# Seven products in place of eight for the first matrix product of two batches, other pairs of token tiles, and a new order of the whole program

## The chip, the cores and the metric

The kernel runs on one core of a Trainium2 chip. The core has a matmul engine (TensorE, PE in the profile, with its weight loads as PEld), three elementwise engines (VectorE or DVE, ScalarE or ACT, GpSimd or POOL) and a queue engine (SyncE, SP) that issues most DMAs. Each engine executes its own instructions strictly in the order in which the program issues them; engines wait for one another by semaphores. The metric is the device time of one execution in microseconds; lower is better.

## The reference

```
q, k, v: (batch 8, heads 12, sequence 448, head size 64), float32
q_n = q / (norm(q) + 1e-6);  k_n = k / (norm(k) + 1e-6)
attn = softmax(q_n @ k_n^T / 0.1)                 # per head, 448 x 448
x = (attn @ v), heads side by side                # 3584 tokens x 768
h = x @ w_in                                      # w_in: 768 x 2048
g = h * clip(h + 3, 0, 6) / 6
out = g @ w_out                                   # w_out: 2048 x 768
```

## The kernel before

Work is done by pairs of heads: 8 batches x 6 pairs = 48, numbered 0 to 47 and called heads below. For each the kernel loads q and k of two heads (`load_qk`, one item j each), squares them (`square`, L228 on ACT, L230 on DVE or POOL), sums the squares (`reduce`, L242), makes the reciprocal norms with four small ACT instructions (`norms`, L258 to L261), scales (`normalise`, L273), transposes by PE or by DMA (`transposes`, `crossbar`), and copies k into a padded tile (`copy_k`, `copy_k3`). `scores` (L418, L421) multiplies keys by queries: the two heads of a pair lie in the upper and lower 64 rows of the array and run side by side, three groups of 128 keys each and a fourth group, M, that holds the last 64 keys of both heads. `exps` (L439, ACT) takes the exponential out of PSUM. `values` (L461) multiplies by the values, which `vcast` turned to bf16 (L292); a column of ones gives the softmax sum, and `finish_values` (L481, L482, DVE) divides. `back_crossbar` and `back_two` transpose the result into `xT`, one of two buffers by batch.

When the six heads of a batch are there, `mm1_unit` (L572) makes the first product for one of 16 blocks of 128 hidden columns: six matmuls of 448 token columns. Its `relu` (L581, ACT) and its gating `product` (L587, DVE) write g.

The second product: batch 0 goes through `mm2_unit` (L619, 16 matmuls of 384 columns). Further tiles of 128 tokens are taken in pairs by Strassen's scheme in Winograd's form: 2 x 2 blocks (two token tiles, two halves of the hidden columns, by two halves of the output columns) need seven products of 8 matmuls in place of eight. `product_unit` (L745) issues one of the products "1" to "7", `g_sum` (L723, DVE) makes a sum of blocks of g (128 x 1024, bf16), `weight_sums` (L694) a sum of blocks of `w_out`, partly in place. ACT and DVE take the results out of PSUM (L764, L770, L793, L802), POOL adds some of them (L774, L775, L778, L786). There are 11 such pairs. Tile 2 of batches 2, 4 and 6 stands alone and goes through `single_unit` (L825, 2 x 16 matmuls).

PSUM has eight banks. After the start, `PV` holds two of them for the values product, and the other six are a ring that score groups and products take in turn (`next_bank`).

The order is written out for heads 0 to 17 in `PLAN`, a list of lines of short words that are executed one after the other (`SC.12.0` is `scores(12, 0)`, `LQ` a load, `DP.5` five filler matmuls by `busy_pv`, L927, `U` the next unit of the products). From head `FIRST` = 18 on a loop issues the work of each head, with the units of the products put between by the tables `TURNS` and `side`. After head 47 the last units follow, `units[NP]`. A finished product leaves two steps in the lists `post`, one for the engine that reads PSUM and one for later, and these are run right behind the unit:

```
def whole_units(n, engines="av"):
    for _ in range(n):
        unit()
        for e in engines:
            while post[e]:
                finish_units(e)
```

Of the kernel before, what the change touches and what calls it, by code (L numbers as in the profile page):

```python
# [8 lines left out]
FP32 = mybir.dt.float32  # L9
# [9 lines left out]
ORDER = "111111111111111111111111111111222222"  # L19

PLAN = [
# [40 lines left out]
def kernel(  # L62
# [49 lines left out]
    qT = [tT[1 + i // 2][:, :, :, :].rearrange("p c n e -> p (c n e)")[:, i % 2 * S : i % 2 * S + S] for i in range(4)]  # L112
    ats = {
        m: [const.tile([128, m, 512], BF16, name=f"at{m}_{i}", tag=f"at{m}_{i}") for i in range(n)]
        for m, n in ((2, 6), (1, 2))
    }
    at_n = {1: 0, 2: 0}
    NV, NR = 3, 7
# [980 lines left out]
```

## Time and profile before

| | |
|---|---|
| median of 3 runs | 405.82 us (404.91 to 405.93) |
| profiled execution, span | 404.0 us (the profile gives its span alone) |
| PE busy | 395.7 us, 98%, 3696 matmuls |
| DVE busy | 288.2 us, 71%, 501 instructions |
| ACT busy | 266.1 us, 66%, 609 instructions |
| POOL busy | 232.7 us, 58%, 228 instructions |
| granted TensorE clock, mean | 0.999 |
| HBM read, written | 47.32 MB, 11.01 MB |

Busy time of an engine counts the union of its instructions' durations. A matmul's duration holds its whole way through the array, and the next one begins long before it ends, so the cost of a matmul in a sequence is its pitch, the time from its start to the next start. The same holds to a smaller extent on ACT and DVE. In a row of a group, "x522 | 110.7, 353 | 0.0" means 522 instructions, 110.7 us of busy time, 353 ns mean duration, and 0.0 us of idle time ahead of them, followed by what ended that idle time.

### The profile page before, as it was taken

How to read it: one execution, taken by the hardware profiler on the slowest of the kernel's cores; microseconds unless marked ns; L12 is line 12 of the kernel's file. 1: busy time of each engine (PE TensorE's matmuls, PEld its weight loads, DVE VectorE, ACT ScalarE, POOL GpSimd, SP SyncE). 2: the span in 40 equal slices, each digit the busy share in tenths (PEclk: the TensorE clock that was granted, in tenths of full speed). 3: DMA queues.
4: the chain of work that ended last, by engine and by line, in shares of the span. 5: the costliest groups of instructions: out<-in, count | busy, mean ns of one | idle time of the engine just before them, and what ended most of it. 6: DMA issues, size and time to landing. Idle time of an engine off the chain costs nothing.

```text
span 404.0 us, 9620 instructions
## 1 busy us (share of the span) xinstructions
PE 395.7 (98%) x3696; PEld 234.0 (58%) x3696; DVE 288.2 (71%) x501; ACT 266.1 (66%) x609; POOL 232.7 (58%) x228
## 2 busy tenths in 40 slices
PE   7999999999989999999999999999999999999996
PEld 4666556555655556555565556555555556555564
DVE  6898768766998676777857887687656666655663
ACT  6899998787567686776758768668647755224230
POOL 7798746662294996588485875776664600510060
PEclk9999999999999999999999999999999999999999
DMA  8999999989989559785989559967864523130033
GB/s 287 278 258 242 223 243 236 186 125 213 206 200 239 113 151 203 173 222 127 181 207 211 125 150 170 188 171 161 198 152 79 112 45 66 38 82 21 22 76 99
DMA packets 91598, 65.45 MB, mean 162 GB/s; under 512 B 56080, under 2 KB 90000, under 8 KB 91536
## 3 DMA queue, kind: packets, MB, share of 16 engines
q1 hardware_dynamic: 87440, 58.15, 63.2%
q0 software_dynamic: 3712, 6.29, 9.0%
q8 instruction: 29, 0.48, 0.5%
q10 hardware_dynamic: 400, 0.39, 0.3%
q14 instruction: 17, 0.14, 0.1%
HBM read 47.32 MB, written 11.01 MB: 144 GB/s over the span
## 4 chain that ended last, share of the span: by engine, by line
PE 94%; DVE 4%; issue 0%; DVEq 0%
PE M L572 23%; PE M L745 17%; PE PV L461 13%; PE Y L572 6%; PE M L421 6%; PE Z L572 5%; PE Z L745 4%; PE Y L745 4%; PE PV L927 3%; PE M L619 3%; PE M L825 2%; PE Z L421 2%; PE Z L825 1%; PE Y L421 1%; PE SC L421 1%; DVE gT L723 1%
## 5 line engine op out<-in xcount | busy, mean ns | idle before, releaser
L439 ACT ACTIVATE at<-M 128x448 bf16<-128x448 f32 x200 | 99.8, 567 | 17.7 <-PE M L421 15.5
L572 PE MATMUL M<-xT,w_in_sb 128*128 128x448 bf16 x522 | 110.7, 353 | 0.0
L572 PEld LDWEIGHTS <-w_in_sb 128*128 128x128 bf16 x768 | 71.9, 98 | 62.6 <-issue 2.6
L273 POOL TENSOR_TENSOR nrm<-big,r 128x896 bf16<-128x896 f32 (+1 forms) x48 | 78.9, 1649 | 21.5 <-ACT r L261 16.2
L587 DVE SCALAR_TENSOR_TENSOR gT<-u,M 128x448 bf16<-128x448 bf16 x76 | 46.8, 618 | 35.5 <-ACT u L581 35.2
L230 POOL TENSOR_TENSOR big<-big 128x896 f32<-128x896 f32 (+3 forms) x39 | 63.4, 1628 | 11.2 <-DVE on L482 6.1
L461 PEld LDWEIGHTS <-at 128*128 128x128 bf16 (+1 forms) x1536 | 54.8, 97 | 24.1 <-issue 14.8
L581 ACT ACTIVATE u<-M 128x448 bf16<-128x448 f32 x87 | 48.8, 561 | 29.6 <-PE M L572 29.2
L461 PE MATMUL PV<-vx,at 128*128 128x65 bf16 (+1 forms) x1536 | 64.4, 194 | 0.2 <-DVE on L482 0.2
L242 DVE TENSOR_REDUCE n<-big 128x14 f32<-128x896 f32 (+1 forms) x50 | 51.8, 1041 | 3.9 <-ACT big L228 3.4
L378 POOL COPY km<-tT 64x128 bf16<-64x128 bf16 x34 | 12.4, 364 | 60.8 <-DMA tT<-nrm 40.8
L774 POOL TENSOR_TENSOR big<-big 128x384 f32<-128x384 f32 x11 | 11.8, 1071 | 55.1 <-ACT big L793 55.0
L745 PEld LDWEIGHTS <-gT 128*128 128x128 bf16 x288 | 27.6, 98 | 20.9 <-DVE gT L723 1.4
L745 PE MATMUL M<-w_out_sb,gT 128*128 128x384 bf16 x208 | 37.9, 326 | 0.1
L292 POOL CAST vx<-big 128x512 bf16<-128x512 f32 x44 | 33.5, 766 | 4.3 <-PE PV L461 2.3
L439 ACT ACTIVATE at<-Z 128x448 bf16<-128x448 f32 x49 | 27.8, 566 | 10.3 <-PE M L421 10.3
L482 DVE TENSOR_TENSOR on<-PV,rc 128x512 bf16<-128x512 f32 x48 | 33.2, 692 | 1.7
L421 PE MATMUL M<-tT,kz 64*128 64x448 bf16 (+1 forms) x175 | 31.9, 351 | 1.0 <-DVE o L632 1.0
L745 PEld LDWEIGHTS <-gs 128*128 128x128 bf16 x224 | 21.6, 98 | 14.6
L572 PE MATMUL Y<-xT,w_in_sb 128*128 128x448 bf16 x132 | 28.6, 353 | 0.0
L439 ACT ACTIVATE at<-Y 128x448 bf16<-128x448 f32 x45 | 25.7, 571 | 3.3 <-PE Z L421 3.1
L745 PE MATMUL M<-w_sum,gs 128*128 128x384 bf16 x144 | 26.4, 326 | 0.0
(131 smaller groups left out, 557.6 us busy)
## 6 DMA issues: line engine op xcount, KB each, us to landing
big<-in_v_dram SPq DMA_DIRECT2D x96, 128.0 KB, 4.4
big<-in_k_dram SPq DMA_DIRECT2D x24, 448.0 KB, 4.7
big<-in_q_dram SPq DMA_DIRECT2D x24, 448.0 KB, 4.4
out_dram<-o SPq DMA_DIRECT2D x107, 96.0 KB, 2.2
w_in_sb<-in_moe_w_in_dram POOLq DMA_DIRECT2D x4, 768.0 KB, 11.0
w_out_sb<-in_moe_w_out_dram POOLq DMA_DIRECT2D x4, 768.0 KB, 9.1
tT<-nrm SPq DMA_TRANSPOSE x34, 3.4
xT<-on SPq DMA_TRANSPOSE x25, 3.9
```

What stands on the lines that cost most here:

```text
L230: engines[e].tensor_tensor(out=o, in0=i, in1=i, op=ALU.mult)
L242: nc.vector.tensor_reduce(out=n2s[d % 2][:, j % 2, c], in_=sq[:, :, :, :].rearrange("p g c d -> p (g c) d")[:, c, :], axis=AX.X, op=ALU.add,)
L273: engines[e].tensor_tensor(out=nrm[:, :, g, :].rearrange("p c g d -> p g c d"), in0=raw_of[j][:, g, :, :], in1=rs[d % 2][3][:, j % 2, :] . ...
L292: (engines[e].copy if e == "a" else engines[e].tensor_copy)(out=o, in_=f)
L421: nc.tensor.matmul(o, ks, qt[rows], start=True, stop=True)
L439: nc.scalar.activation(out=o, in_=x, func=AF.Exp, scale=inv_tau)
L461: nc.tensor.matmul(pv_out(j, h), at[rows, n, q_cols(i // HP, j)], vt[rows, 3 + h if name == "M" else 5 * h + int(name[1]), :], start=(name ...
L482: nc.vector.tensor_tensor(out=on[:, :, :, :].rearrange("p j h d -> p h j d"), in0=pv4[:, :, :, 0:D], in1=rc[:, :, :].to_broadcast([128, 2, ...
L572: nc.tensor.matmul(ps[:, 0:S], w_in_sb[:, cc, fc * 128 : (fc + 1) * 128], x[:, cc, 0:S], start=(cc == 0), stop=(cc == CC - 1),)
L581: nc.scalar.activation(out=u[:, :], in_=ps[:, 0:S], func=AF.Relu, bias=0.5, scale=1.0 / 6.0)
L587: nc.vector.scalar_tensor_tensor(out=g[:, fc, c0 : c0 + S], in0=u[:, :], scalar=1.0, in1=ps[:, 0:S], op0=ALU.min, op1=ALU.mult,)
L745: nc.tensor.matmul(m, lhs[:, c, :], rhs[:, c, c0 : c0 + width], start=(base is None and c == 0), stop=(c == KC - 1), skip_group_check=True,)
```

## The change

1. *First product of batches 6 and 7.* After head 47 the first product of these two batches is no longer made by `mm1_unit`. The 448 tokens are split in two halves of 224, the 768 inputs in two of 384 (three chunks of 128), the hidden columns in two of 1024. `in_sum` makes five sums of halves of `w_in` (three into a free part of the buffer `big`, two in place), `x_sum` five sums of halves of `xT`. For each n of 8, `quad_first`, `quad_second` and `quad_third` issue the seven products, 21 matmuls of 224 columns: products 4, 3 and 1 first; ACT keeps their results in SBUF (`keep`), POOL adds (`add`); products 2 and 5 are accumulated on 4 and 3 and give two quarters of the result; DVE subtracts the bank from the kept sums into another bank (`rest`), on which 6 and 7 are accumulated for the other two quarters. Activation and gating follow as before, per two quarters.
2. *Banks at the end.* `tail_banks` closes `PV` when head 47 is done and makes its two banks the ring for the second product; the six others serve the seven products (three for 4 and 3, two for 6 and 7, one for 1). `wide_ring` joins all when the last group is issued.
3. *Pairs across batches.* The token tiles of all batches form one sequence, without the first two, and are paired in that order, so tile 2 of batches 2, 4 and 6 pairs with a neighbour of the next batch. There are 13 pairs, no `single_unit`, and four `mm2_unit`.
4. *One order.* The loop, `TURNS`, `side` and the units are gone; `PLAN` has 96 lines and names each operation and its engine: the products (`F`, `P`, `T`, `QA`, `QB`, `QC`), the steps behind them (`FA`, `FV`, `PE`, `BO`, `RS`, `PL`, `QK`, `QD`, `QR`, `QU`, `QV`), and the sums (`G`, `WS`, `IS`, `XS`). 40 of the 65 sums of g name POOL; squares, normalisations and value casts change engines too. Fillers are 64 in three places, for 96 in many. The dummy loads of `stagger` are not in the list. In 44 of the 48 heads `values` takes group M at half height (`.h`), side by side for the two heads; before, these were heads 18 to 47.
5. *Buffers.* The tiles `at` become one tile, `att`, parts of which hold sums and kept results at the end. g of batch 7 stays in `gT`.

The diff, cut:

```
 PLAN = [
...
+    "LQ.0 SQ.0.a.8.6 SQ.0.a.0.6 SQ.0.v.6.2 RE.0.1 RE.0.0 LQ.1 SQ.1.a.0.4 SQ.1.p.4.3 SQ.1.v.7.4 SQ.1.a.11.3 RE.1.1 RE.1.0 LQ.3 NO.0.0 NM.0.p.0 SQ.3.v.0.7",
+    "LQ.2 NO.0.1 NM.1.v.0 NM.1.p.1 DP.58 TR.1.Y NM.0.p.1 RE.3 TR.0.Z SQ.2.a.0.7 CK.0.a CK.1.a RE.2 NO.1 CQ.0.v LQ.6 LQ.4 CQ.1.v SQ.4.v.0.7 RE.4 NM.3.v LQ.5",
+    "SQ.5.p.0.7 RE.5 NM.2.p DP.1 SC.0.0.0 LV.0 VC.1.v SC.0.1.1 EX.0.0 EX.0.1 LQ.7 DP.5 SC.0.2.0 SC.0.3.1 EX.0.2 EX.0.3 SC.1.0.0 EX.1.0 LV.1 LQ.8 VC.0.p",
...
+    "CQ.10.v CQ.11.v F.0.0 FA.0.0 FI.6 FV.0.0 SC.8.0 SC.8.1 EX.8.0 EX.8.1 F.0.3 LQ.15 SC.8.2 SC.8.3 VC.7.v F.0.1 FA.0.3 EX.8.2 NM.11.p FV.0.3 FA.0.1 W.3",
...
+    "G.1.0.p G.6.0.p G.2.0.p P.2.0.a NO.11 LQ.25 LV.10 LQ.26 CK.20.v WS.1 NM.22.v CK.21.v LV.11 LQ.27 FA.2.4 VC.19.a PE.3.0.a PL.5.0 FA.2.6 FA.2.5 FV.2.4",
...
+    "PE.1.8.v EX.46.0 EX.46.1 VA.45.3.h SC.46.2 XP.42 VA.45.2 VA.45.1 FI.45 P.6.8 EX.46.2 RS.8 CS.46.v SC.46.3 EX.46.3 VA.46.0 PE.6.8.v SC.47.0 SC.47.1",
+    "SC.47.2 VA.46.3.h EX.47.0 EX.47.1 EX.47.2 VA.46.1 VA.46.2 SC.47.3 EX.47.3 XS.6.2.v FI.46 XB.46 P.7.8 PE.7.8.v VA.47.0 VA.47.2 VA.47.1 IS.3.p VA.47.3.f",
+    "FI.47 TB XS.6.1.p QA.6.0 QK.6.0 QA.6.1 XS.6.5.p QD.6.0 QK.6.1 QB.6.0 QD.6.1 QU.6.0.1 QR.6.0 QV.6.0.1 QA.6.2 QK.6.2 QB.6.1 QU.6.1.1 QR.6.1 QV.6.1.1",
+    "QB.6.2 QU.6.2.1 QC.6.0 QU.6.0.2 QV.6.0.2 QA.6.3 QK.6.3 QD.6.2 QR.6.2 QV.6.2.1 QC.6.1 QU.6.1.2 QD.6.3 QV.6.1.2 QB.6.3 QU.6.3.1 QV.6.3.1 QR.6.3 QA.6.4",
...
+    "P.5.12 PE.5.12.v BO.12 P.7.12.1 P.3.11 P.1.12 PE.4.11.a PE.3.11.a G.1.11.v G.5.11.v P.5.11 P.2.11 G.6.12.v G.2.12.v PE.1.12.v P.2.12 PE.7.12.1.v",
+    "PE.2.11.v PE.2.12.a PE.5.11.v P.7.11.2 P.1.11 BO.11 RS.11 PE.7.12.0.v PE.1.11.v PE.7.11.v RS.12 P.6.12.2 PE.6.12.v P.6.11.2 PE.6.11.v",
 ]
...
-    def values(i, g):
-        needs(("VC", i), ("FI", i - 1), *values_after(i, g))
+    def values(i, g, rows_of="f"):
+        needs(("VC", i), ("FI", i - 1), *([("VA", i, 0)] if g else []))
...
-                    rows = slice(64 * h, 64 * h + 64) if name == "M" and i >= FIRST else slice(0, 128)
+                    rows = slice(64 * h, 64 * h + 64) if name == "M" and halves else slice(0, 128)
...
-    PAIRS = [p for b in range(0, B, 2) for p in (((b, 0), (b, 1)), ((b + 1, 3), (b + 1, 0)), ((b + 1, 1), (b + 1, 2)))][1:]
-    LOOP = 8
+    TILES = [x for b in range(0, B, 2) for x in ((b, 0), (b, 1), (b, 2), (b + 1, 3), (b + 1, 0), (b + 1, 1), (b + 1, 2))][2:]
+    PAIRS = list(zip(TILES[::2], TILES[1::2]))
+    LOOP = 10
...
-        nc.vector.tensor_tensor(out=o[:, :, :], in0=x, in1=y, op=op)
+        engines[e].tensor_tensor(out=o[:, :, :], in0=x, in1=y, op=op)
...
+    def tail_banks():
+
+        n = ring_n[0]
+        older = [ring[(n + x) % len(ring)] for x in range(len(ring))]
+        needs(("FI", NP - 1))
+        QUAD["pq"] = [b for b in older if id(b) not in narrow][:2]
+        rest = [b for b in older if not any(b is x for x in QUAD["pq"])]
+        QUAD["xy"], QUAD["r"] = rest[:3], rest[3:]
...
+    def quad_product(b, n, name, o, start=False):
...
+        for c in range(KX):
+            nc.tensor.matmul(
+                o, lhs[:, c, :], rhs[:, c, :], start=start and c == 0, stop=c == KX - 1, skip_group_check=True
+            )
+
+    def quad_first(b, n):
...
+        quad_product(b, n, "4", xy[:, 0:SX], True)
+        quad_product(b, n, "3", xy[:, SX:S])
+        quad_product(b, n, "1", r[:, 0:SX], True)
+
+        def keep():
+            nc.scalar.copy(out=t[:, 0:2, :], in_=xy[:, 0:S].rearrange("p (m n) -> p m n", m=2))
+            nc.scalar.copy(out=t[:, 2, :], in_=r[:, 0:SX])
...
+        def add():
+            nc.gpsimd.tensor_tensor(out=t[:, 0, :], in0=t[:, 0, :], in1=t[:, 1, :], op=ALU.add)
+            nc.gpsimd.tensor_tensor(out=t[:, 2, :], in0=t[:, 0, :], in1=t[:, 2, :], op=ALU.add)
...
+    def quad_second(b, n):
...
+        quad_product(b, n, "2", xy[:, 0:SX])
+        quad_product(b, n, "5", xy[:, SX:S])
+
+        def rest():
...
+            nc.vector.tensor_tensor(
+                out=pq[:, 0:S].rearrange("p (m n) -> p m n", m=2),
+                in0=bass.AP(tensor=f.tensor, offset=f.offset, ap=[f.ap[0], [0, 2], [1, SX]]),
+                in1=xy[:, 0:S].rearrange("p (m n) -> p m n", m=2),
+                op=ALU.subtract,
+            )
...
+        activated(b, n, 1, xy, ((n, 1), (n + FCN // 2, 0)))
+
+    def quad_third(b, n):
...
+        quad_product(b, n, "6", pq[:, 0:SX])
+        quad_product(b, n, "7", pq[:, SX:S])
+        activated(b, n, 2, pq, ((n + FCN // 2, 1), (n, 0)))
```

More of the change, by code (lines that the diff above doesn't have):

```diff
@@ L295 @@
     unread = {}
+    narrow = set()
     def bank_of(name, reads):
@@ L429, in exps @@
         at = ats[m][at_n[m] % len(ats[m])]
+        assert not any(x is at for x in at_of.values())
         at_n[m] += 1
@@ L612, in mm2_unit @@
     def mm2_unit(b, t, m):
-        assert not weights and ("y4", "y3")[m] not in [x for x, _ in summed]
+        assert len(weights_in) == len(weights) and ("y4", "y3")[m] not in [x for x, _ in summed]
         complete(b, t)
+        t_read.add((b, t, m))
+        if (b, t, 1 - m) in t_read:
+            g_read.add((b, t))
         g = g_of(b)
         ps, key = bank_of(None, 1)
+        narrow.add(key)
         cols = slice(m * MH, m * MH + MH)
@@ L753, in product_unit @@
         issued_products.add((n, name))
+        if all((n, x) in issued_products for x in "2345") and all((n, x) in g_summed for x in "167"):
+            g_read.update(PAIRS[n])
         d, e = d_and_e(n)
@@ L876 @@
-    units = {}
-    carry = firsts(1, FCN - 2, FCN - 1)
-    for b in range(2, B - 1):
-        first = firsts(b, *range(FCN))
-        for n, x in enumerate([0, 3, 3, 3, 3, 2]):
-            i = (b + 1) * HP + n
-            u = carry + [first.pop(0) for _ in range(x)]
-            carry = []
-            *p, last = products(TURNS[i])
-            if i == NP - 1:
-                p, last = [last], None
-            x = 0 if n == 1 else 1 if n in (0, 5) and i > FIRST else 2
-            units[i] = u[:x] + p + u[x:]
-            units[i] += [last] if last else []
-        carry = first
@@ new lines, in x_half, with x_sum @@
+    def x_half(b, t, k):
+        return xT[b % 2][:, KX * k : KX * k + KX, SX * t : SX * t + SX]
+    def x_sum(b, what, e="v"):
+        a11, a12, a21, a22 = (x_half(b, t, k) for t in range(2) for k in range(2))
+        for w in {"2": "6", "5": "7"}.get(what, ""):
+            assert (b, w) in x_summed
+        o, x, y, op = {
+            "6": (a21, a21, a11, ALU.subtract),
+            "2": (a21, a21, a22, ALU.add),
+            "7": (a12, a12, a22, ALU.subtract),
+            "5": (a12, a12, a11, ALU.add),
+            "1": (a11, a11, a22, ALU.add),
+        }[what]
+        if what in "167":
+            o = x_sums[b][what]
+        engines[e].tensor_tensor(out=o, in0=x, in1=y, op=op)
+        x_summed.add((b, what))
@@ L966, in run @@
         for t in text.split():
+            key = t.rstrip("avp").rstrip(".")
+            if key in later:
+                later.pop(key)(*([t[-1]] if t[-1] in "avp" else []))
+                continue
             op, *args = t.split(".")
```

403 lines of the change are left out of this document (219 added, 184 removed), and 126 rows, old and new, of tables (PLAN, TURNS).

## The prediction

> **What bounds the kernel now.** I read the page first, then the stage table, the timeline of single stretches and the groups by shape.
>
> ```profile
> span 404.0 us, 9620 instructions
> PE 395.7 (98%) x3696; PEld 234.0 (58%) x3696; DVE 288.2 (71%) x501; ACT 266.1 (66%) x609; POOL 232.7 (58%) x228
> ```
>
> The median of the runs, 405.82, lies 1.8 us over the profiled span; I make every sum against 404.0 and add 1.8 at the end. TensorE (PE) looks full, but a busy PE may be doing fillers. The stage tables (the first over all, the next two over the fillers alone):
>
> ```profile
> 0.00:60.00 60.00, 57.03 (x673) 36.56 (x674) 46.42 (x115) 52.47 (x111) 45.47 (x53) 1.00 1.06 254
> 60.00:320.00 260.00, 258.49 (x2467) 150.69 (x2467) 194.66 (x309) 183.55 (x438) 172.26 (x161) 1.00 0.81 175
> 320.00:404.00 84.00, 80.19 (x563) 46.78 (x559) 47.11 (x77) 30.06 (x62) 14.97 (x16) 1.00 0.25 57
> 0.00:42.50 42.50, 13.79 (x86) 8.22 (x86) 1.00 1.04 268
> 0.00:42.50 42.50, 3.02 (x10) 1.25 (x10) 1.00 1.04 268
> ```
>
> The columns are PE, weight loads, DVE, ACT, POOL (for the fillers PE and weight loads alone), then clock, DMA share and GB/s. Fillers hold PE for 13.8 + 3.0 us of the first 42.5. From 60 us on PE is full to 99%, and in the last 84 us ACT is used at 36% and POOL at 18%: there is room for added elementwise work at the end, and none on PE. Matmul durations overlap, so I take pitches, start to start, from the chain and from timelines of PE:
>
> ```profile
> 2.47 3.90 PE PV L927 x18
> 9.18 1.38 PE PV L927 x13
> 363.15 3.40 PE M L572 x18
> 376.77 5.20 PE M L825 x32
> 257.60 0.36 PE L421 MATMUL Y<-tT,kz 64*128 64x448 bf16 x1
> 257.90 0.66 PE L461 MATMUL PV<-vx,at 128*128 128x65 bf16 x16
> 258.40 0.33 PE L745 MATMUL Z<-w_sum,gs 128*128 128x384 bf16 x1
> 36.19 0.36 PE L421 MATMUL Z<-tT,kz 64*128 64x448 bf16 x1
> 36.39 0.65 PE L421 MATMUL M<-tT,kz 64*128 64x448 bf16 x3
> L461 PE MATMUL PV<-vx,at 64*128 64x65 bf16 x240 | 8.8, 193 | 0.0
> ```
>
> A 448-column matmul costs 3.40/18 = 0.189 us, a 384-column one 5.20/32 = 0.1625, a 65-column one 0.50/16 = 0.031; a pair of half-height score matmuls 36.39 - 36.19 = 0.20. Going from half height to full costs 0.30 - 0.20 = 0.10 extra (257.60 to 257.90). Useful PE work now: 768 first-product matmuls x 0.189 = 145; second product 808 x 0.1625 = 131; values and scores some 42 + 37; transposes 8; about 150 changes of height x 0.1 = 15: 378 us. PE's last matmul ends near 400, so about 22 us are no useful work: 2.5 before the first, most of 17 in fillers, some 5 in scattered waits. The last 4 us are a drain:
>
> ```profile
> 399.37 0.82 PE L745 MATMUL Z<-w_sum,gs 128*128 128x192 bf16 x8
> 400.23 0.36 DVE L770 TENSOR_TENSOR o<-Z,big 128x192 f32<-128x192 f32 x1 [0.24 <-PE Z L745]
> 396.95 4.35 SPq L607 DMA_DIRECT2D out_dram<-o  x5
> ```
>
> **The change, part by part: PE.**
> - First product of batches 6 and 7. Out: 192 x 0.189 = 36.3. In: 16 groups x 21 matmuls of 224 columns. From 448 and 384 columns the slope is 0.414 ns a column, so 224 cost 0.096: 336 x 0.096 = 32.2. Gain 4.1. The weights change with each matmul, but the 65-column row shows a change of weights every 0.031, so loads do not limit 0.096.
> - Token tiles in pairs across batches: 13 pairs x 56 + 4 plain units x 16 = 792 for 808. Gain 16 x 0.1625 = 2.6.
> - Last key group of the values product at half height in 44 heads for 30 (the x240 row is 30 heads x 8): 14 x (8 x 0.031 - 4 x 0.033) = 1.6 gained. Counting heights along the new PE order gives about 6 more changes: 0.6 lost.
>
> Sum on PE: -7.7. All of it is on the path, since PE ends last.
>
> **Start.** The first exponential runs at 12.4:
>
> ```profile
> 12.44 2.54 ACT L439 ACTIVATE at<-SC 128x896 bf16<-128x896 f32 x3 [0.75 <-PE SC L421]
> 14.84 0.24 ACT L258 ACTIVATE ln<-n 128x28 f32<-128x28 f32 x1
> 35.29 0.36 PE L421 MATMUL M<-tT,kz 64*128 64x448 bf16 x2
> 42.49 2.38 PE M L572 x12
> 37.45 1.42 ACT L439 ACTIVATE at<-M 128x448 bf16<-128x448 f32 x3
> 38.72 0.59 ACT L439 ACTIVATE at<-Z 128x448 bf16<-128x448 f32 x1
> ```
>
> New: item 0 loads first, its squares go to ACT and DVE, 58 fillers run ahead of the first transpose (18 at 0.207, 40 at 0.106: to 10.4), then the chain square, reduce, four norm steps, normalise, transpose, copy has the same length. I take 12.4 again (11.5 to 13.5). Now six heads take 12.4 to 35.3 before head 6 begins. New: several squares of this stretch go to POOL and DVE, so ACT has 18 x 0.80 + 6 x 0.42 and about 4 us of norms and copies, 21 us: head 6 at 33 to 36. Then comes a debit: the first product of batch 0 now starts behind head 7's exponentials, not at 42.5. Between heads 6 and 12 the lists give PE 26.6, ACT 26.7 (0.423 for each 448-column exponential, from 37.45 and 38.72) and DVE 24.4: three engines level, so waits show. I book 0 for the start, from -3 to +4. The loads on SP's queue keep their number and change places, and two dummy loads fall out:
>
> ```profile
> big<-in_k_dram SPq DMA_DIRECT2D x24, 448.0 KB, 4.7
> ```
>
> At 254 GB/s one item takes 1.8 us; items 4 and 5, sixth and seventh in the queue, land near 15 and are wanted for head 4 at about 25: covered.
>
> **Middle.** Sums of the second product, squares and normalisations change engines. The rows:
>
> ```profile
> L230 POOL TENSOR_TENSOR big<-big 128x896 f32<-128x896 f32 x36 | 60.4, 1680 | 10.0 <-DVE on L482 6.1 <-DMA big<-in_q_dram 1.5 <-DVE n L242 1.3
> L273 POOL TENSOR_TENSOR nrm<-big,r 128x896 bf16<-128x896 f32 x44 | 75.3, 1713 | 20.8 <-ACT r L261 15.5 <-issue 5.2
> L292 POOL CAST vx<-big 128x512 bf16<-128x512 f32 x44 | 33.5, 766 | 4.3 <-PE PV L461 2.3 <-DMA big<-in_v_dram 2.0
> L774 POOL TENSOR_TENSOR big<-big 128x384 f32<-128x384 f32 x11 | 11.8, 1071 | 55.1 <-ACT big L793 55.0
> 178.25 2.20 DVE L723 TENSOR_TENSOR gs<-gT 128x1024 bf16<-128x1024 bf16 x1
> 328.98 0.68 DVE L723 TENSOR_TENSOR gs<-gT 128x1024 bf16<-128x1024 bf16 x1
> 178.22 1.68 POOL L230 TENSOR_TENSOR big<-big 128x896 f32<-128x896 f32 x1 [0.86 <-DMA big<-in_q_dram]
> 179.86 2.14 POOL L273 TENSOR_TENSOR nrm<-big,r 128x896 bf16<-128x896 f32 x1
> ```
>
> POOL takes 40 of the 65 sums. No row has such a sum on POOL: the normalisation's rate (1.713/896) gives 1.96 us, the 384-wide add's (1.071/384) 2.86; I take 2.5, nearer the add, which is the same operation. So POOL: 232.7 + 40 x 2.5, - 19 squares x 1.68, - 17 normalisations x 1.71, - 24 casts x 0.77, + 32 adds of 224 x 0.65, + 2 weight sums of 3072 (7 each), + 7 token sums of 672 (1.6 each) = about 300 us, 76%. DVE gets 14 squares and 17 normalisations and loses 33 sums: about 325 us, 82%. Neither total reaches PE's, but 76 of DVE's instructions are of the kind that takes turns with POOL: one sum lasts 0.68 alone and 2.20 when it begins with a POOL operation (178.25 against 178.22 + 1.68). Queued behind it on DVE are the gating products, which free PE's banks. Between heads 18 and 22 the lists give PE 30.1, POOL 31.3, DVE 27.8 plus ten such turns: level again. Against this stand the 5 us of scattered waits of now. I book +0.5 (bounds -3 and +8).
>
> **End.** After the last value product PE has 68.5 us left, now 60. A group of the seven products needs ACT to keep three results, POOL two adds, DVE a subtraction into the bank of products 6 and 7, then two activations and three gating products. Per group, from
>
> ```profile
> L439 ACT ACTIVATE at<-M 128x448 bf16<-128x448 f32 x200 | 99.8, 567 | 17.7 <-PE M L421 15.5 <-PE Y L421 1.8
> L587 DVE SCALAR_TENSOR_TENSOR gT<-u,M 128x448 bf16<-128x448 bf16 x76 | 46.8, 618 | 35.5 <-ACT u L581 35.2
> ```
>
> ACT 3 x 0.42 + 0.24 = 1.5, DVE about 1.9, POOL 1.3, PE 21 x 0.096 = 2.0: PE still longest. But product 1 has one bank: PE issues products 4 and 3 of the next group (0.57) while ACT still copies three results (0.06 + 0.42 + 0.34), so 0.25 is open in each of the eight groups of batch 6, which have nothing else beside them: 2 us. Product 1 of the first group also waits for a token sum that stands on POOL behind a 7 us weight sum; POOL's list from head 42 to there is 34.9 us, PE's 33.9: 1 us. The drain grows 0.3, because the last two products are full width. End: +3.3. Where these stalls are avoided, the rest of the end still covers 51 us of POOL by 49 of PE, so POOL is next. Of the present waits I let about 3 go (weight sums and left columns that PE now meets later in the order).
>
> Sum: 404.0 - 7.7 + 0 + 0.5 + 3.3 - 3 = 397.1; with 1.8, **399.0 us**. Its own range is 395 to 404.
>
> **Rivals.**
> 1. *The order also saves idle time.* Fewer fillers (64 for 96) and evener engines: waits of the middle down to 2, end to 2, start -3. 404.0 - 7.7 - 3 - 3 + 2 = 392.3, time 394. For it: DVE 71% and POOL 58% now; against: the level sums above. 22%.
> 2. *Slower: DVE and POOL take turns in the middle.* Place: heads 12 to 36 and the end. 76 turns x 0.9 us (half a POOL operation of 1.7 to 2.5, at 76% busy) is some 50 us of DVE. Slack on DVE is 70. It decides once more than 7 us of these 50 reach PE through a late gating product; at 10 to 12 us the time is 408. For it: 178.25. Against: that sum of 2.20 held up no matmul in the chain. [...] 20%.
> 3. *The clock falls.* PE has gaps between 12 and 35 us that 32 more fillers hold closed now; the same filler took 0.207 cold and 0.106 warm. About 17 us of work at half rate in 23 us is 10 us late: 407. All stage rows of now read 1.00, so no fall is seen; gaps there would be under 2 us. 4%. [...]
> 4. *The seven products do nothing*: were 224 columns to cost 0.14 for 0.096, the 4.1 would be lost and the time be 406 with waits as now. The 65-column row speaks against it. 4%.
>
> **How the numbers follow.** My forecast has 50%. About 0.3%, 1.2 us, is what a measurement can tell from no change. Faster (below 404.6) is nearly all of the forecast and rival 1: 70%; same 8%; slower 22%, from rivals 2 to 4. The range goes from 391.5 (rival 1 with every bound low) to 407 (into rival 2).
>
> **What would show it.** Right: 336 matmuls of 224 columns at a pitch of 0.096; 792 for the second product; PE's useful work 370; head 6 by 36 us; the clock row all nines; PE waits of some 0.25 in batch 6's groups and a total of waits near that of now. Wrong: POOL sums of 2.9 or more, DVE rows two or three times their lone length right before PE waits, first exponentials after 14, or POOL at 9 through the last 70 us with PE waiting for its adds.

## The result and the profile after

| | before | after |
|---|---|---|
| median | 405.63 us (404.91 to 405.93) | 449.07 us (448.19 to 450.43) |
| ratio | | 1.1078 (95% interval 1.1049 to 1.1107) |
| span of the profiled execution | 404.0 us | 448.7 us |

The change costs 43 us; 399.0 was predicted, within 391.5 to 407.0. In experiments 1, 6, 8 and 14 one of four executions was in a slower state of the chip, and the time given is the median of the other three. First the page of the changed kernel: the engines, the slices of PE, DVE, POOL and the clock, and the shares of the chain that ended last.

```profile
span 448.7 us, 10043 instructions
PE 401.3 (89%) x3792; PEld 246.6 (55%) x3792; DVE 354.2 (79%) x552; ACT 289.7 (65%) x659; POOL 315.6 (70%) x257
...
PE   7758999998977879999699999999897979989985
...
DVE  7697896879897766776978869877877976985883
...
POOL 6794826317798948879736269288978996979642
PEclk9697999999996969999989999999989999999999
...
PE 45%; DVE 18%; POOL 16%; DMA 8%; issue 7%; ACT 4%; SPq 1%; POOLq 0%; DVEq 0%; ACTq 0%
```

No engine is full. Of the chain, PE has 45%; DVE and POOL carry 34% of it. The stage table of the changed kernel, and below it the fillers alone (columns as before):

```profile
0.00:60.00 60.00, 47.95 (x547) 30.64 (x548) 49.37 (x104) 44.45 (x98) 41.07 (x47) 0.89 0.88 226
60.00:320.00 260.00, 242.65 (x2250) 137.91 (x2247) 206.61 (x304) 181.60 (x420) 175.46 (x131) 0.97 0.75 168
320.00:448.70 128.70, 110.74 (x1007) 78.00 (x1003) 98.23 (x146) 63.67 (x144) 99.04 (x80) 0.99 0.28 63
...
0.00:42.50 42.50, 8.57 (x64) 6.77 (x64) 0.84 0.94 251
```

PE is idle for 12.1, 17.4 and 18.0 us of the three stages (3.0, 1.5 and 3.8 before), and the granted clock fell to 0.89 and 0.97 in the first two. PE's busy time hides a part of the loss, since rows grew where the clock was lower: between 16 and 25 us the score matmuls of 448 columns average 0.450 us at a clock of 0.65, where before the change they average 0.360 at 1.00. So I add up along each trace what every matmul but the fillers costs by the prediction's prices; the time up to a point less this sum is what PE has lost by then:

| | useful | lost by 60 us | 60 to 320 | behind 320 |
|---|---|---|---|---|
| before | 375.2 | 19.3 | 5.1 | 0.3 |
| after | 368.0 | 28.4 | 29.2 | 17.9 |

The work on PE fell by 7.2 us. Lost time rose by 9.1, 24.1 and 17.6: together +43.6 (spans +44.7; the missing 1 us is the drain behind PE's last matmul, 3.8 before and 4.8 after). By the list of waits, some 30 of PE's 42 us of waiting in the changed kernel end with an instruction of DVE, 8 with one of POOL and 3 with one of ACT. The next lines are POOL's two longest waits and PE's longest (total, times, longest), and then two groups of POOL and four of DVE, by shape:

```profile
POOL nrm L335 <- ACT r L323: 20.3, 6, 6.5
...
POOL gs L824 <- DVE gT L671: 16.6, 4, 7.1
...
PE M L849 <- POOL gT L824: 7.2, 3, 5.3
```

```profile
L824 POOL TENSOR_TENSOR gT<-gT 128x1024 bf16<-128x1024 bf16 x15 | 35.1, 2343 | 1.4 <-DVE gs L824 0.6
...
L824 POOL TENSOR_TENSOR gs<-gT 128x1024 bf16<-128x1024 bf16 x14 | 31.8, 2275 | 19.1 <-DVE gT L671 13.5
```

```profile
L671 DVE SCALAR_TENSOR_TENSOR gT<-u,M 128x448 bf16<-128x448 bf16 x64 | 38.3, 614 | 18.2 <-ACT u L665 18.0
...
L335 DVE TENSOR_TENSOR nrm<-big,r 128x896 bf16<-128x896 f32 x18 | 28.1, 1561 | 4.1 <-DMA tT<-nrm 3.8 <-ACT r L323 0.2
L292 DVE TENSOR_TENSOR big<-big 128x896 f32<-128x896 f32 x13 | 23.7, 1823 | 0.1
L824 DVE TENSOR_TENSOR gT<-gT 128x1024 bf16<-128x1024 bf16 x11 | 16.9, 1542 | 0.1
```

The same sums before the change:

```profile
L723 DVE TENSOR_TENSOR gT<-gT 128x1024 bf16<-128x1024 bf16 x18 | 17.1, 951 | 0.6
```

DVE's gating products (one operand in PSUM) keep their 0.61, but the normalisations, squares and sums, which read both operands from SBUF, average 1.56, 1.82 and 1.54 where the shortest of each last 1.07, 1.07 and 0.68. Over all groups of DVE, the time above the shortest of the same shape is 22.7 us before and 59.0 after. Two places in the timeline of the changed kernel show what holds DVE, and who waits for it:

```profile
26.72 5.22 DVE L292 TENSOR_TENSOR big<-big 128x896 f32<-128x896 f32 x1
31.86 0.68 DVE L403 COPY tT<-Y 128x448 bf16<-128x448 bf16 x2
...
26.53 1.18 POOL L354 CAST vx<-big 128x512 bf16<-128x512 f32 x2
27.66 1.68 POOL L292 TENSOR_TENSOR big<-big 128x896 f32<-128x896 f32 x1
29.31 1.68 POOL L335 TENSOR_TENSOR nrm<-big,r 128x896 bf16<-128x896 f32 x1
30.94 1.47 POOL L354 CAST vx<-big 128x512 bf16<-128x512 f32 x1
...
32.59 0.58 PE L559 MATMUL Y<-ident,on 128*128 128x128 bf16 x4 [3.60 <-DVE tT L403]
...
362.29 5.03 DVE L1021 TENSOR_TENSOR xT<-xT 128x672 bf16<-128x672 bf16 x1
...
360.96 5.99 POOL L1001 TENSOR_TENSOR w_in_sb<-w_in_sb 128x3072 bf16<-128x3072 bf16 x1
...
368.22 0.95 PE L521 MATMUL PV<-vx,att 128*128 128x65 bf16 x26 [3.04 <-DVE on L542]
```

At 26.72 a square of 1.07 lasts 5.22. Four instructions of POOL run meanwhile, three of which began after it; only the fifth, the cast at 30.94, is late itself (1.47 for 0.60). The copy of the queries behind the square is late, PE idles 3.60 us, and the clock row falls to 7 in the next slice (34 to 45 us). At 362.29 a token sum (0.77 at its shortest) begins 1.3 us into POOL's weight sum of 5.99 and ends 0.4 us behind its end, and PE gets its values product 3.04 us late. In the middle it is POOL's own length; this is the chain from 120 to 138 us:

```profile
120.52 2.80 POOL gs L824
123.32 0.07 issue
123.39 2.72 POOL gT L824
126.11 3.15 POOL big L292
129.26 5.67 POOL gs L824 x2
...
135.02 2.85 POOL gT L824
```

POOL works without a gap, and PE waits 5.26 us at 132.6 for the last of these sums.

### The profile page after: what moved, and what is told of

Same layout as the page of the kernel before. It is cut to its first block, busy times and chain, and to the rows that moved or that the text cites. A ratio compares the mean times of both kernels' runs of the same rounds, so it can differ in the third digit from the quotient of the medians.

```text
span 448.7 us, 10043 instructions
## 1 busy us (share of the span) xinstructions
PE 401.3 (89%) x3792; PEld 246.6 (55%) x3792; DVE 354.2 (79%) x552; ACT 289.7 (65%) x659; POOL 315.6 (70%) x257
## 4 chain that ended last, share of the span: by engine, by line
PE 45%; DVE 18%; POOL 16%; DMA 8%; issue 7%; ACT 4%; SPq 1%; POOLq 0%; DVEq 0%; ACTq 0%
PE M L656 10%; PE M L849 9%; PE PV L521 5%; POOL gs L824 5%; PE V L849 4%; PE Y L849 3%; PE M L485 3%; DMA big<-in_k_dram 2%; POOL gT L824 2%; DVE n L304 2%; PE Y L656 2%; PE Z L656 2%; DMA big<-in_q_dram 2%; PE M L1038 2%; DMA tT<-nrm 2%
## 5 line engine op out<-in xcount | busy, mean ns | idle before, releaser
L504 ACT ACTIVATE att<-M 128x448 bf16<-128x448 f32 x193 | 96.3, 558 | 18.2 <-PE M L485 15.5
L335 POOL TENSOR_TENSOR nrm<-big,r 128x896 bf16<-128x896 f32 (+1 forms) x31 | 54.2, 1757 | 39.9 <-ACT r L323 20.3
L521 PEld LDWEIGHTS <-att 128*128 128x128 bf16 (+1 forms) x1536 | 57.3, 99 | 30.2 <-issue 16.2
L521 PE MATMUL PV<-vx,att 128*128 128x65 bf16 (+1 forms) x1536 | 66.1, 196 | 5.2 <-DVE on L542 4.5
L292 POOL TENSOR_TENSOR big<-big 128x896 f32<-128x896 f32 (+1 forms) x20 | 34.9, 1748 | 34.9 <-DVE n L304 12.8
L665 ACT ACTIVATE u<-M 128x448 bf16<-128x448 f32 x64 | 35.2, 556 | 17.9 <-PE M L656 17.4
L824 POOL TENSOR_TENSOR gs<-gT 128x1024 bf16<-128x1024 bf16 x14 | 31.8, 2275 | 19.1 <-DVE gT L671 13.5
L485 PE MATMUL M<-tT,kz 64*128 64x448 bf16 x171 | 34.6, 361 | 5.3 <-DVE gT L671 4.5
L824 POOL TENSOR_TENSOR gT<-gT 128x1024 bf16<-128x1024 bf16 x15 | 35.1, 2343 | 1.4 <-DVE gs L824 0.6
L849 PE MATMUL M<-w_sum,gs 128*128 128x384 bf16 (+1 forms) x176 | 31.6, 322 | 3.4 <-DVE big L912 2.8
L504 ACT ACTIVATE att<-Z 128x448 bf16<-128x448 f32 x53 | 29.7, 561 | 5.3 <-PE M L485 2.7
L335 DVE TENSOR_TENSOR nrm<-big,r 128x896 bf16<-128x896 f32 (+1 forms) x19 | 29.4, 1550 | 4.1 <-DMA tT<-nrm 3.8
```

What stands on the lines that cost most here:

```text
L292: engines[e].tensor_tensor(out=o, in0=i, in1=i, op=ALU.mult)
L335: engines[e].tensor_tensor(out=nrm[:, :, g, :].rearrange("p c g d -> p g c d"), in0=raw_of[j][:, g, :, :], in1=rs[d % 2][3][:, j % 2, :] . ...
L485: nc.tensor.matmul(o, ks, qt[rows], start=True, stop=True)
L504: nc.scalar.activation(out=o, in_=x, func=AF.Exp, scale=inv_tau)
L521: nc.tensor.matmul(pv_out(j, h), at[rows, n, q_cols(i // HP, j)], vt[rows, 3 + h if name == "M" else 5 * h + int(name[1]), :], start=(name ...
L665: nc.scalar.activation(out=u[:, :], in_=ps[:, 0:S], func=AF.Relu, bias=0.5, scale=1.0 / 6.0)
```

## The experiments

Theory A is the prediction's second rival: the instructions that moved between DVE and POOL cost more than their lengths, and PE waits for them; A1 says through DVE being held up, A2 through POOL's own lengths. Theory B is that the new order leaves no slack, whatever the engines. Theory C is the clock.

**1. The sums back on DVE.**

```
- G.7.0.p  G.5.0.p  G.1.0.p ...
+ G.7.0.v  G.5.0.v  G.1.0.v ...      (all 40)
```

> The changed kernel with the 40 sums of g that POOL makes put back on DVE; nothing else moves. Theory A (turns): DVE's two-input instructions are shut out by POOL's; POOL loses 40 x 2.3 = 93 us of such work, DVE gains 40 x 0.7 = 28, its time over lone length falls from 59 us to some 30: time 415 to 430. Theory B (order): the new order has no slack whatever the engines: 440 or more. Theory C (start and clock): the 9 us more that are lost before 60 us stay, the rest stays too: 445.

439.70 us, ratio 1.0787 (1.0699 to 1.0875). POOL falls from 315.6 to 221.4 us, DVE hardly changes (354.2 to 348.1): what it gets back it had lost in held-up instructions, whose added length falls from 59 to 28 us. Only 9 of 43 us come back, less than A named and about what B did. In the profiled execution (span 434.3) PE loses 5.5, 4.1 and 4.2 us less in the three stages. The first 5.5 are not the edit's: POOL's first sum runs at 120.48, so up to 60 us the two kernels are the same. In this execution the square that stands at 26.72 above ran beside POOL's issue of a DMA and took its usual 1.08, and the clock of the first stage stayed at 1.00. In the kernel of experiment 6, which has the same start, it is as before:

```profile
24.72 1.08 DVE L292 TENSOR_TENSOR big<-big 128x896 f32<-128x896 f32 x1
...
27.56 5.19 DVE L292 TENSOR_TENSOR big<-big 128x896 f32<-128x896 f32 x1
```

So what the start of the changed kernel loses can differ by some 5 us from one execution to the next.

**2. Squares and normalisations back on POOL as well.**

```
- SQ.j.v  NM.j.v  G.x.n.p
+ SQ.j.p  NM.j.p  G.x.n.v
```

> As the run with the sums on DVE, and also DVE's 17 squares and 19 normalisations on POOL, so that the three kinds of work stand on the engines that had them before; the order of the words is that of the changed kernel. Theory A: DVE's time over lone length falls to 25 us or less, as before; POOL 315 - 93 + 36 x 1.65 = 282: time 400 to 415. Theory B: 440 or more. If POOL's own length then counts (normalisations of 1.7 for 1.1 on the way to the scores of the first heads): slower than the run with the sums on DVE alone, in the first 60 us.

452.09 us, 1.1127 (1.1045 to 1.1209): no gain over the change, though POOL is busy for 60% and DVE for 71% (58% and 71% before the change), and DVE's added length is back at 27 us. So the holding of DVE is not the whole cost. The engines of before do not repair an order that was made for other engines. This speaks for B, but weakly, since the two were never meant for each other.

**3. More fillers.**

```
  SC.i.g ...
+ DP.2          (behind each SC of heads 0 to 5)
```

> The changed kernel with two filler matmuls behind each score group of heads 0 to 5 (48 more). Theory C: the granted clock of the first 40 us rises from 0.77 to 0.88 to about 1, and the time falls by 3 to 6 us: 443 to 446. Theory A: DVE and ACT set the pace there; the clock rises, and the time stays within 2 us.

446.88 us, 1.0985 (1.0920 to 1.1050). The clock rises from 0.962 to 0.985 and 2 us come back. So the low clock is not what costs most of the 43 us. That it follows from the waits is read from the two rows at 26.72 and in the clock row, and not tested.

**4. and 5. The old order with the new engines.** First 40 of the 58 sums on POOL alone (the expectation's 37 is a miscount of mine; POOL has 40 such rows), then half of the squares and normalisations on DVE as well.

```
- nc.vector.tensor_tensor(out=o[:, :, :], in0=x, in1=y, op=op)
+ e = nc.gpsimd if what in ("7", "5", "6") or (what == "1" and n > 3) else nc.vector
+ e.tensor_tensor(out=o[:, :, :], in0=x, in1=y, op=op)
...
- prepare(("SQ", i + 5, "p", 0, 7))
+ prepare(("SQ", i + 5, "v" if i % 2 else "p", 0, 7))
...
- prepare(("NM", i + 3, "p"), ...
+ prepare(("NM", i + 3, "p" if i % 2 else "v"), ...
```

> The kernel before, its order unchanged, with 37 of its 58 sums of the second product on POOL and nothing else moved (squares and normalisations stay on POOL); with half of those moved to DVE as well it took 427.3. POOL then has 233 + 37 x 2.3 = 318 us, DVE 288 - 25 = 263 and only 21 sums and the weight sums that read two operands from SBUF. Theory A1 (shut-outs on DVE): there is little left to shut out, 412 or less. Theory A2 (POOL's own length and its full queue): 418 or more.

> The kernel before, its order and its products unchanged, with 37 of its 58 sums of g on POOL (products 7, 5, 6, and 1 of the later pairs) and, in the loop, every other square and every other normalisation on DVE. Theory A: the mix of engines alone costs tens of us in the old order as well: 425 to 450, DVE's time over lone length 50 or more. Theory B: under 412, since the order is the old one.

426.64 us, 1.0492 (1.0432 to 1.0552), and 427.26, 1.0508 (1.0449 to 1.0567). Moving the sums costs 5% in an order that runs at 98% on PE with them on DVE, and moving squares and normalisations the other way adds nothing. A1 named 412 or less for the first, since few instructions of DVE are left that could be held up, and it is wrong there; A2 holds. DVE's added length, counted as above, is 23 and 25 us in the two, no more than the 22.7 of before; the second expectation had named 50 or more, so its time came, but not by its mechanism. The page and a group of the kernel with the sums on POOL:

```profile
PE 402.6 (95%) x3696; PEld 235.0 (55%) x3696; DVE 264.3 (62%) x461; ACT 266.4 (63%) x609; POOL 313.3 (74%) x268
```

```profile
L724 DVE TENSOR_TENSOR gT<-gT 128x1024 bf16<-128x1024 bf16 x9 | 14.8, 1639 | 17.9 <-POOL gs L724 13.1 <-POOL big L724 4.8
```

DVE has lost load (62%), and it now idles for POOL: a sum of 2.12 us in front of another that needs it, where both stood in one queue at 0.68 each.

**6. and 7. Short instructions on POOL.** Most of the length is taken away from 27 of POOL's 40 sums, and in the second kernel from its squares from item 4 and its normalisations from item 6 as well; that work is left out. The instructions, waits and places stay.

```
+ k = 1 if e == "p" and n not in (0, 1, 10, 11) else KC
- engines[e].tensor_tensor(out=o[:, :, :], in0=x, in1=y, op=op)
+ engines[e].tensor_tensor(out=o[:, 0:k, :], in0=x[:, 0:k, :], in1=y[:, 0:k, :], op=op)
```

and in the second kernel the same in the squares and the normalisations (one slot of seven).

> The changed kernel, with 27 of the 40 sums that POOL forms for the second product cut to their first 128 of 1,024 columns (the rest of the sum is left out, so its result is not the product). Every instruction, wait and place in the order stays; POOL loses 27 x 2.3 x 7/8 = 54 us of its 316. Theory A (what costs the time is POOL's long sums, by their own length and by what they hold up on DVE): the time falls by 25 us or more, to 424 or less, below what giving these sums back to DVE reached (440.5). Theory B (the order of the instructions on each engine, whatever their length): 440 or more.

> As the kernel with the short sums, and the squares from item 4 on (19) and the normalisations from item 6 on (25) that POOL forms are cut to one of their seven slots too (the rest of them is left out, so later results are not the attention's). POOL then works for about 195 us of the 316, and holds DVE up hardly at all; the order and every wait stay. Theory A: all of the 43 us between the two kernels comes from what POOL does and holds up, so the time is 410 or less, and the DVE rows return to their lengths alone. Theory B: the order keeps PE waiting with a nearly idle POOL too, 430 or more. Between them, the share of each is read off.

432.82 us, 1.0627 (1.0557 to 1.0697), halfway between the two theories, and 414.16, 1.0201 (1.0169 to 1.0233), near A. With POOL at 202.7 us in the unchanged new order, 35 of the 43 us are gone.

**8. and 9. The mirror, and both.** The same cuts on DVE's squares, normalisations and sums alone (`e == "v"`), then on both engines.

> The mirror of the kernel with everything short on POOL: now DVE's squares (from item 4 on), normalisations (from item 6 on) and those sums of the second product that stay on DVE are cut to a seventh or an eighth (the rest is left out, so later results are wrong), POOL keeps its full lengths, and every instruction, wait and place stays. These are the rows that grew on DVE (88 us in the changed kernel, of which 38 are above their length alone). Theory A1 (the time goes where POOL holds up DVE's instructions with two operands in SBUF, and DVE then comes late for PE): 420 or less. Theory A2 (the time goes into POOL's own lengths, 2.1 to 2.5 us for a sum, waited for directly): 437 or more.

> Squares, normalisations and sums cut on DVE and on POOL alike (the rest of them is left out); the order and all waits stay. What is left above PE's useful 368 us and the 24.6 us that the kernel before loses is the order's own. If everything beside the start came from DVE and POOL: 400 or less. If the order alone costs some 10 us: 405 to 412, little below the 414 that the short POOL reached.

424.37 us, 1.0493 (1.0367 to 1.0619), and 407.32, 1.0021 (0.9994 to 1.0048). Short on POOL takes away 35 us, short on DVE some 25, both 42: each way cuts into the same waits. These cuts do not part A1 from A2, since with POOL's cut (experiment 7) DVE is held for less too (its normalisations, squares and sums average 1.38, 1.21 and 1.05 for 1.56, 1.82 and 1.54), and a short one on DVE also saves its own length. Experiment 4 shows A2 with no more holding than before, and experiment 11 the holding with no work saved. In the kernel with DVE cut, DVE's short pieces last far longer than their work:

```profile
L338 DVE TENSOR_TENSOR nrm<-big,r 128x128 bf16<-128x128 f32 x17 | 13.0, 762 | 5.8 <-DMA tT<-nrm 5.6 <-ACT r L325 0.2
...
L828 DVE TENSOR_TENSOR gT<-gT 128x128 bf16<-128x128 bf16 x7 | 6.8, 970 | 0.1
```

The shortest of these rows last 0.28 and 0.21; the mean is 0.76 and 0.97. The stages with both cut:

```profile
0.00:60.00 60.00, 52.66 (x642) 33.67 (x642) 50.57 (x118) 51.71 (x119) 25.64 (x51) 0.97 1.05 246
60.00:320.00 260.00, 255.41 (x2438) 148.42 (x2438) 179.81 (x322) 193.41 (x446) 105.75 (x145) 0.99 0.77 176
320.00:406.30 86.30, 80.05 (x720) 61.29 (x716) 58.04 (x112) 42.52 (x96) 60.71 (x62) 0.99 0.24 56
```

By the same count PE loses 20.3, 10.1 and 2.8 us: 8.5 more than before the change, and this is the most that is left for B (weight sums, token sums and the sums of four pairs keep their length), next to the 7.2 us of work that were saved. The new order, freed of nearly all two-operand work on both engines, ties with the old one that has it in full.

**10. The hold by itself.** Behind the end of the old kernel, DVE's square, sum, reduction and copy stand alone and then beside POOL's instructions issued back to back (this stretch is no part of the computation).

```
+ for p, n in ((p_square, 0), (p_square, 8), (p_sum, 8), (p_cast, 16)):
+     for d in (d_square, d_sum, d_reduce, d_copy):
+         together(d, p, 4, n)
```

> The kernel before, with a stretch behind its end (not part of the computation): DVE's square (896 f32), sum (1,024 bf16), reduction (896 f32) and copy (1,024 bf16), four of each, first alone, then beside POOL's squares, sums and casts issued back to back. If a DVE instruction that reads two operands from SBUF is shut out while POOL has work in a row: squares and sums of several us, as long as POOL's row of instructions, the reduction 1.07 as alone. If the two engines only take turns instruction by instruction: at most alone plus one POOL instruction, 2.8 for the square and 2.4 for the sum. POOL's own rows should be 1.68 (square), 2.12 (sum), 0.61 (cast) where they come first.

The rows of that stretch: DVE alone (404 to 418 us), then beside POOL's squares.

```profile
404.04 4.47 DVE L1072 TENSOR_TENSOR big<-big 128x896 f32<-128x896 f32 x4
408.62 2.86 DVE L1075 TENSOR_TENSOR big<-big 128x1024 bf16<-128x1024 bf16 x4
411.54 4.44 DVE L1078 TENSOR_REDUCE big<-big 128x14 f32<-128x896 f32 x4
416.03 1.80 DVE L1081 COPY big<-big 128x1024 bf16<-128x1024 bf16 x4
418.02 7.19 DVE L1072 TENSOR_TENSOR big<-big 128x896 f32<-128x896 f32 x4
419.23 16.30 POOL L1084 TENSOR_TENSOR big<-big 128x896 f32<-128x896 f32 x8
...
435.71 5.58 DVE L1075 TENSOR_TENSOR big<-big 128x1024 bf16<-128x1024 bf16 x4
...
451.79 4.44 DVE L1078 TENSOR_REDUCE big<-big 128x14 f32<-128x896 f32 x4
...
466.44 4.52 DVE L1081 COPY big<-big 128x1024 bf16<-128x1024 bf16 x4
```

In each set of four the first two run before POOL has begun. The two that meet POOL last 2.45 for 1.09 (square; 7.19 is about 2 x 1.09 + 2 x 2.45), 2.05 for 0.69 (sum) and 1.78 for 0.43 (copy); the reduction stays at 1.09. POOL's squares beside DVE's last 2.41 for 1.68 (two of them take 4.89). So it is the second of the two expectations: in this stretch the engines alternate, one instruction each, and a turn costs both lengths less some 0.3 us. The 5.22 at 26.72 does not occur in this stretch, but it is no accident of one execution: the same square lasts 5.19, 5.24 and 6.05 in experiments 6, 14 and 11, and 1.93 and 1.08 in 3 and 1, where it began at another point of POOL's row. Why it lets several instructions of POOL pass stays open. The runs show the lengths alone; what in the chip makes one engine wait for the other they do not show.

**11. Shorter instructions on POOL, the same work.**

```
- engines[e].tensor_tensor(out=o[:, :, :], in0=x, in1=y, op=op)
+ h = KC // 2 if e == "p" else KC
+ for k in range(0, KC, h):
+     engines[e].tensor_tensor(out=o[:, k : k + h, :], in0=x[:, k : k + h, :], in1=y[:, k : k + h, :], op=op)
```

and so for squares, normalisations (four and three slots) and the two weight sums (six pieces).

> The changed kernel with POOL's long instructions cut into shorter ones that do the same work: each sum of 1,024 as two of 512, squares and normalisations as four and three slots of seven, the two weight sums of 3,072 as six of 512. From the stretch of measurements, DVE's two-operand instruction waits for the POOL instruction in progress and then the two alternate, and a POOL sum of 128 columns lasts 0.42 us beside 2.12 for 1,024, so a cut adds about 0.18 us: some 90 cuts, 16 us more on POOL. If the length of the POOL instruction in progress is what costs DVE: the rows on DVE lose a third of their 36 us of added length, and the time falls to 430 to 442. If DVE alternates with more, shorter instructions and POOL's total decides: 447 to 460.

439.76 us, 1.0834 (1.0802 to 1.0866): 9 us less, as the first of the two expectations has it, with 18 us more work on POOL (333.8) and nothing left out. The rows of DVE get shorter, as these three of that kernel show beside 1561, 1823 and 1542 above:

```profile
L338 DVE TENSOR_TENSOR nrm<-big,r 128x896 bf16<-128x896 f32 x18 | 25.2, 1398 | 3.3 <-DMA tT<-nrm 3.0 <-ACT r L325 0.2
L294 DVE TENSOR_TENSOR big<-big 128x896 f32<-128x896 f32 x13 | 20.3, 1563 | 3.2 <-DMA big<-in_q_dram 2.2 <-DMA big<-in_k_dram 0.9
L829 DVE TENSOR_TENSOR gT<-gT 128x1024 bf16<-128x1024 bf16 x11 | 15.3, 1391 | 1.1 <-POOL gs L829 1.0
```

DVE's added length falls from 59 to 35 us, by two thirds of its rise, where one third was named. It is mainly the length of the POOL instruction in progress that DVE pays for; the square that lets several pass (6.05 here) is the exception.

**12. and 13. The old start, alone and with the sums on DVE.** All tokens up to the opening of the ring come from the old list.

```
- LQ.0 SQ.0.a.8.6 ... (new start)
+ LQ.1 DP.5 SQ.1.a.11.3 ... OPEN (old start), the rest in the new order
```

> The changed kernel with the start of the kernel before: all that the old order issues up to the opening of the ring behind head 5 (items 0 to 11, heads 0 to 5, fillers, dummy loads, the engines of these squares and normalisations) takes the place of what the new order issues of the same work, and the rest follows in the new order. By 60 us the changed kernel had lost 28.4 us of PE's time and the kernel before 19.3. If the start is a cost of its own: 440 (9 us less). If lost time there is only moved, since later stages wait for the same engines anyway: within 3 us of 449.

> The changed kernel with two parts put back: the old start (alone: 8 us less) and all sums of the second product on DVE (alone: 9 us less). If these two losses are separate, as their places in the trace are (before and after 60 us): 432. If both come back elsewhere: 438 or more. Under 425 would say that they hinder each other.

441.18 us, 1.0871 (1.0833 to 1.0909), and 437.30, 1.0770 (1.0724 to 1.0817). By 60 us PE has lost 20.6 us, about the old 19.3; the 8 us stay gained to the end. They do not add up with the 9 us of the sums: together 12, nearer to the 438 of the second case than to 432.

**14. Without the seven products.**

```
- QA.b.n  QB.b.n  QC.b.n ...  IS.x  XS.b.x
+ F.b.n FA.b.n FV.b.n  F.b.(n+8) FA.b.(n+8) FV.b.(n+8)
```

> The changed kernel with the seven products of batches 6 and 7 taken out again: each head chunk of the first product as six full matmuls, one activation and one gating product, no token sums, no weight sums for it, no copies and additions of partial results; all else in the new order and on the new engines. PE's useful work rises by 4.1 us. By the prediction's sum (a gain of 4.1 on PE, 3.3 lost again at the end): 450. If the elementwise work that the seven products bring (about 35 us on POOL, 25 on DVE and ACT each) is what the last 125 us wait for, where 18 us were lost: 440 or less.

444.81 us, 1.0946 (1.0873 to 1.1019). Its gating products stand where the first ones of the seven products stood, and the edit also keeps the old ring of banks to the end and lets it pass over banks not yet read. The time lies between the two named. PE has 4 us more work here and still ends earlier: the seven products cost at least as much, through their elementwise work or through the banks, as they save. Behind 320 us PE loses about 7 us less than in the changed kernel, of the 17.6 that had been added there; the rest of the end's loss has other causes.

**15. One part of the change in the old order.**

```
- rows = ... if name == "M" and i >= FIRST else ...
+ rows = ... if name == "M" and (i >= FIRST or i in (4, 5, 7, 8, 9, 11, 14)) else ...
```

> The kernel before with one part of the change alone: the last key group of the values product at half height in heads 4, 5, 7, 8, 9, 11 and 14 too, where a half-height product stands beside it on PE, so that no change of height is added. By the prediction's size, 7 x (8 x 0.031 - 4 x 0.033) = 0.8 us of PE work less: 405.2 where PE is the bound there, 406.0 where the start's waits take it up.

405.25 us beside 405.47, 1.0001 (0.9975 to 1.0027). The count of useful work, which takes the prediction's prices, falls from 375.2 to 374.6; the gain is too small to be seen in the time, so the price of a half-height group is not tested by it. No version here beats the kernel before.

## Why the prediction was wrong

- **PE, -7.7: right as work.** The count of matmuls at the prediction's prices gives -7.2. There are 336 matmuls of 224 columns, at a pitch of 0.0958 (twelve steps from 385.54 to 386.69); the price 0.096, the one new one, held. "All of it is on the path, since PE ends last" did not hold: PE has 45% of the chain.
- **Start, booked 0, bounds -3 to +4: wrong, +9.1.** The first exponential runs at 13.37 (12.4 taken, 11.5 to 13.5 allowed), head 6 at 43.1 where 33 to 36 was said. The sentence "I take 12.4 again" was good to 1 us; what failed is that "several squares of this stretch go to POOL and DVE" was booked as a relief for ACT, without what they do to each other: the square of 5.22 stands here (and in one execution it does not, experiment 1). The old start wins this back on the chip.
- **Middle, booked +0.5 from -3 to +8: the step that failed, +24.1.** Its sizes were near: a POOL sum alone 2.12 (2.5 taken), a weight sum 6.0 (7), a token sum 1.45 (1.6), POOL 315.6 (about 300). DVE came to 354.2 for 325 (the terms listed for DVE give only about 299; the elementwise work of the seven products is not among them), and the 29 that were missing lie within the 36 us by which its added length rose. The error is in the next step, that level totals show few waits and that "Neither total reaches PE's". The sums stand in chains (gating product, POOL sum, second sum, product) in queues that are worked in order (the copy of the queries, whose transposes ended at 28.10, ran at 31.86, behind the square); a total says nothing of that. In its place the runs showed that POOL's lengths, and what they hold on DVE, make up most of the loss: 35 of the 43 us go when POOL's instructions are short, 42 when DVE's are short too.
- **End, booked +3.3: wrong, +17.6.** By the same count PE loses about 12 us between 320 and 369, ahead of the seven products, 3.5 while they run (to 421) and 2.5 behind them. So the stalls I looked for inside the groups were about as small as booked, and most of what was missed stands ahead of them, where the sums of `w_in`, of tokens and of g share the two engines. PE's longest wait there (3.04) is the values product behind the token sum of 5.03, which POOL's weight sum holds. That weight sum was seen ("a token sum that stands on POOL behind a 7 us weight sum") and priced at 1 us as a place in POOL's queue, not as a hold on DVE.
- **Rival 2** named the mechanism (DVE and POOL take turns, heads 12 to 36 and the end) and priced the work well: some 50 us on DVE, measured 36 above before. It then let "10 to 12 us" reach PE. Some 35 to 42 did, because it left out that POOL's instructions grow too (its sums average 2.28 and 2.34 for 2.12) and are waited for directly, which the sums on POOL in the old order show by themselves (+21). It was given 20% and a time of 408 (by its own terms 408.4 to 410.4), and nothing held a longer tail.
- **Rival 1** did not occur. **Rival 3**: the clock did fall, to 0.89 by 60 us, by my reading as a follower of the waits, which no run tests (PE's gap at 32.6 is 3.60 us, where under 2 was said); fillers brought 2 us. **Rival 4**: the price of 224 columns held; whether the saving survives its elementwise work is not settled by experiment 14, which changes the banks too; there it does not.
- **The 3 us of present waits that were to go** can't be told apart under losses of this size.
- One count of the prediction was off without effect on its sum: the trace before has 70 changes from half to full height, not about 150, and the useful work comes to 375.2 us, not 378.
- The row that should have decided was in the prediction: 178.25, a sum of 2.20 for 0.68. The words "that sum of 2.20 held up no matmul in the chain" were true of a kernel where DVE's two-operand work was mostly sums with room around them. Their use as an argument against the rival was the mistake: the change takes that room away.

What stays open: how the up to 8.5 us of the order itself arise, why the square at 26.72 let several instructions of POOL pass, and how the parts divide, since they overlap (25 and 35 for 42).

## What to carry to other kernels

Moving elementwise work between DVE and POOL was not moving load between two free engines here: in the changed kernel the 25 sums left on DVE average 1.46 us where the shortest lasts 0.68, and POOL's 40 average 2.34 where the shortest lasts 2.12. My estimate where the two meet, from the sets of experiment 10 (2.45 for a square of 1.09 beside one of 1.68): price each two-operand SBUF instruction on DVE at its own length plus one POOL instruction of those beside it, and a POOL instruction that meets one on DVE likewise (2.41 there), and then follow who stands behind both in the queues. Where POOL must do long work next to DVE, try it cut into short instructions (9 us less in experiment 11). And a saving on PE of 2% (here 7.2 us, and the time rose by 43) is worth nothing until the chain that feeds PE has been followed with the new lengths; equal totals below PE's are no evidence for cover.

## What was unexpected of the hardware

- DVE's instructions with two SBUF operands, and its copy from SBUF to SBUF in bf16, lasted longer where they met POOL's. Beside squares of 1.68 (experiment 10) a square took 2.45 for 1.09, a sum 2.05 for 0.69, the copy 1.78 for 0.43; in the changed kernel a token sum, 0.77 at its shortest, took 5.03 and ended 0.4 us behind the weight sum of 5.99 that it met. Reductions kept their 1.09 in experiment 10, and gating products, with an operand in PSUM, their 0.61 in the changed kernel.
- The holding was mutual: POOL's square of 1.68 lasted 2.41 beside DVE's (experiment 10).
- Cut to a seventh or an eighth (experiment 8), DVE's pieces of the two rows shown still averaged 0.76 and 0.97 us where the shortest last 0.28 and 0.21: the shorter instructions were held all the same. Cutting POOL's instructions into shorter ones (experiment 11), with all their work, brought DVE's normalisations from 1.56 to 1.40.
- The turns were not always one for one: a square of 1.07 lasted 5.2 to 6.1 us behind four to six POOL instructions in four runs, and 1.08 in another execution of the same start.
